# Queries and keys from batch 2 on: cast in DRAM and transposed by DMA instead of by TensorE, and a wider gap between output tiles of the second layer

## The chip, the cores and the metric

The kernel runs on one core of one Trainium2 chip. The metric is the device time of one execution in microseconds (us). A core has TensorE (PE in the profile, its weight loads PEld), VectorE (DVE), ScalarE (ACT), GpSimd (POOL) and SyncE (SP), which here only issues DMAs; each works through its own instructions in order and waits on semaphores for the others. A lower time is better.

## The reference

Attention with a bias by relative distance, then a two-layer network with a squared ReLU:

```python
B, H, S, D = 8, 8, 576, 64             # batches, heads, positions, head size
scores = q @ k.T / 8 + bias_table[bucket(|i - j|)]      # per batch and head
attn = exp(scores - max) / sum
x = (attn @ v), heads side by side      # 4608 tokens x 512
h = maximum(x @ w_in, 0)                # 512 -> 2048
out = (h * h) @ w_out                   # 2048 -> 512, float32
```

Inputs are float32; the kernel computes in fp16 with float32 sums.

## The kernel before

A batch is handled as four pairs of heads and two halves of 288 queries. `run(h)` issues one half: h = 0 to 15, batch h // 2, half ic = h % 2. For each pair it walks a list of slots. There are five score slots (four blocks of 128 keys and one of 64: TensorE writes the transposed scores `st` to PSUM, ScalarE takes the exponential to `et` or `em`, VectorE multiplies a band near the diagonal by the bias table), two slots for the product with v (`pv`) of the pair before, and, in the second half of a batch, one slot "t" that prepares the same pair of the next batch. After each slot `feed` issues pieces of the two network layers, by due times in steps, 28 steps to a half: `ffn1` (line 354, tiles `hps`, ReLU `rt` by ScalarE, square into `g_sb` by VectorE) and `ffn2` (line 376). An output tile of `ffn2` is 16 matmuls into the one PSUM tile `yps`, issued two at a time in eight pieces; VectorE then scales it to `y` (line 382), which frees `yps` for the next tile, and SP stores it. The due times of the eight pieces leave `F2_GAP` steps between the last piece of one tile and the first of the next (`layer2`).

Everything of one engine is issued in the order of this program, so a late operand stops all that stands behind it on that engine.

How q and k come in: SP loads both as float32 with heads side by side (`load_qk`, line 112: ten DMAs a batch with 256-byte rows). GpSimd casts them to fp16 tiles `qh` and `kh` (`cast_qk`, line 162; 32 casts a batch), one half ahead of their use. In slot "t", `transposes(p)` has TensorE transpose five blocks of q and five of k into one of the two PSUM slots that the scores also use (line 235), and VectorE copies the result out in four pieces (lines 238 to 241): q to `qt`, and k to `kz`, where the two heads of a pair lie in different partitions with zeros beside them, so that one 128-row matmul gives one head's scores. v is loaded by SP and cast by GpSimd piece by piece (`cast_v`, line 169); the casts of w_out for the second layer (line 196) stand in h = 2. The memory pools: `qt` five slots, `kz` five tiles, score PSUM two slots, `yps` one.

Of the kernel before, what the change touches and what calls it, by code (L numbers as in the profile page):

```python
# [13 lines left out]
FP16 = mybir.dt.float16  # L14
# [6 lines left out]
B, H, S, D = 8, 8, 576, 64  # L21
# [6 lines left out]

STEP, AFTER1, AFTER2 = 28, 9, 3

F2_GAP = 2.0
F2_PACE = STEP * 16 / 288
F2_START = 5 * STEP + AFTER1 + AFTER2 - 48 * F2_PACE
TILES = [(0, 1), (2, 3), (4, 5), (6, 7, 8)]
# [15 lines left out]
def kernel(  # L50
# [10 lines left out]
    nc = tc.nc  # L61
    assert (_bucket(np.arange(128, S)) == NBK - 1).all()

    def io(ins):
        tc.keep_in_program_order(ins)
        return ins
# [5 lines left out]
    eye = np.eye(128, dtype=np.float16)  # L72
    id_d = nc.inline_tensor(np.concatenate([eye, eye[::-1]], axis=1), name="c_id")
    tdram = nc.dram_tensor("t_bias", (H, 512), FP16, kind="Internal")

    single = ctx.enter_context(tc.tile_pool(name="single", bufs=1))
    stg_pool = ctx.enter_context(tc.tile_pool(name="stg", bufs=1))
    ws_pool = ctx.enter_context(tc.tile_pool(name="ws", bufs=4))
    qt_pool = ctx.enter_context(tc.tile_pool(name="qt", bufs=5))
    et_pool = ctx.enter_context(tc.tile_pool(name="et", bufs=11))  # L80
    nr_pool = ctx.enter_context(tc.tile_pool(name="nr", bufs=2))
    em_pool = ctx.enter_context(tc.tile_pool(name="em", bufs=3))
    xt_pool = ctx.enter_context(tc.tile_pool(name="xt", bufs=2))
    rt_pool = ctx.enter_context(tc.tile_pool(name="rt", bufs=3))
# [22 lines left out]
    kzs = [single.tile([128, 2 * S], FP16, name=f"kz{i}") for i in range(5)]  # L107
# [3 lines left out]
    def sdma(eng, out_, in_):  # L111
        io(eng.dma_start(out=out_, in_=in_))  # L112


    stgs = {}

    def stage(b, names):
        stgs.setdefault(b, [None] * 3)
        for n in names:
            stgs[b]["qkv".index(n)] = stg_pool.tile([128, 5, 512], FP32, tag=n + "s", name=n + "s")  # L120

    def load_qk(b, h0, n, w, eng=nc.sync):
        t, src = stgs[b][w], (q, k)[w]
        for tt in range(4) if n > 2 else ():
            sdma(
                eng,
                t[:, tt, ds(64 * h0, 64 * n)].rearrange("p (h d) -> p h d", d=D),
                src[b, h0 : h0 + n, ts(tt, 128), :].transpose([1, 0, 2]),
            )
        for h in range(h0, h0 + n) if n <= 2 else ():  # L130
            sdma(eng, t[:, 0:4, ts(h, D)], src[b, h, 0:512, :].rearrange("(t p) d -> p t d", p=128))
        sdma(
            eng,
            t[0:64, 4, ds(64 * h0, 64 * n)].rearrange("p (h d) -> p h d", d=D),
            src[b, h0 : h0 + n, 512:576, :].transpose([1, 0, 2]),
        )

    def load_v(b):
        vs = stgs[b][2]
        for tt in range(4):  # L140
            sdma(
                nc.sync,
                vs[:, tt, :].rearrange("p (h d) -> p h d", h=8),
                v[b, :, ts(tt, 128), :].transpose([1, 0, 2]),
            )
        for e in range(2):
            sdma(
                nc.sync,
                vs[ds(64 * e, 64), 4, :].rearrange("p (h e d) -> p h e d", e=2, d=64)[
                    :, :, e, :  # L150
                ],
                v[b, e::2, 512:576, :].transpose([1, 0, 2]),
            )
# [36 lines left out]
    def load_w_out(u):  # L190
        ws[u] = ws_pool.tile([128, 2, 512], FP32, tag="ws", name="ws")
        sdma(nc.sync, ws[u], moe_w_out[ds(u * 256, 256), :].rearrange("(a p) c -> p a c", p=128))
# [22 lines left out]
    def table(hp):  # L215
        for e in range(2):
            tp = psF.tile([128, 512], FP32, tag=f"f{e + 1}", name="tbp")
            io(
                nc.tensor.matmul(
                    tp[:, 0:384], flip_sb, tr[hp // 2][:, 2 * (hp % 2) + e, :], start=True, stop=True  # L220
                )
            )
            io(nc.vector.tensor_copy(out=tb_sb[:, 2 * hp + e, :], in_=tp[:, 0:384]))
            io(nc.gpsimd.tensor_copy(out=tm_sb[ds(64 * e, 64), hp, :], in_=tb_sb[0:64, 2 * hp + e, 0:192]))


    qts, ets, bands = {}, {}, []

    def transposes(p):
        b, hp = divmod(p, 4)  # L230
        qh, kh = h16s
        tp = psS.tile([128, 2, 1024], FP16, tag="s", name="tp")
        for w, src in ((0, qh), (1, kh)):
            for t in range(5):
                io(nc.tensor.transpose(tp[:, w, ts(t, 128)], src[:, t, ts(hp, 128)], id_sb))  # L235
        qt = qt_pool.tile([128, S], FP16, tag="qt", name="qt")
        kz = kzs[p % 5]
        io(nc.vector.tensor_copy(out=kz[0:64, 0:S], in_=tp[0:64, 1, 0:S]))
        io(nc.vector.tensor_copy(out=qt, in_=tp[:, 0, 0:S]))
        io(nc.vector.tensor_copy(out=kz[64:128, S + 64 : 2 * S], in_=tp[64:128, 1, 0:512]))  # L240
        io(nc.vector.tensor_copy(out=kz[64:128, S : S + 64], in_=tp[64:128, 1, 512:S]))
        qts[p] = (qt, kz)
# [151 lines left out]
    def layer2():  # L394
        for h in range(2 * B):
            for _ in ffn2(h):
                nq[0] += 1
                m, n = divmod(nq[0], 8)
                yield F2_START + 8 * m * F2_PACE + n * (8 * F2_PACE - F2_GAP) / 7

# [6 lines left out]
    def feed(t):  # L407

        while streams:
# [11 lines left out]
            name=nc.get_next_instruction_name(),  # L421
# [12 lines left out]
    for h0 in (2, 4):  # L434
        for w in range(2):
            load_qk(0, h0, 2, w)
# [49 lines left out]
    def run(h):  # L486

        nonlocal pending
        b, ic = divmod(h, 2)
        slots = []  # L490
        for hp in range(4):
            p = 4 * b + hp
            slots.append(("unit", hp))
            slots += [("s", p, jt, ic) for jt in range(3)]
            nt = p + 1 if h == 0 and hp < 3 else p + 4 if ic == 1 and b + 1 < B else None
            if nt is not None and h > 0:
                slots.append(("t", nt))
            if h == 0 and hp == 1:
                slots.append(("table",))
            slots += [("pv",), ("pv",)]  # L500
            if nt is not None and h == 0:
                slots.append(("t", nt))
            slots += [("s", p, jt, ic) for jt in range(3, 5)]
            slots.append(("end", p, ic))
        n_real = sum(s_[0] not in ("end", "unit", "table") for s_ in slots)
        at = 0
        for s_ in slots:
            if s_[0] == "end":
                pending = pv(s_[1], s_[2])
                continue  # L510
            if s_[0] == "table":
                for i in range(4):
                    table(i)
                    for p, f in [x for x in bands if x[0] == i]:
                        f()
                bands.clear()
                continue
            if s_[0] == "unit":
                hp = s_[1]
                if b + 1 < B:  # L520
                    if ic == 0 and b > 0 or ic == 1 and b == 0:
                        for w in range(2):
                            for e in range(2):
                                cast_qk(b + 1, w, 2 * hp + e, 1, nc.gpsimd)
                if h in (0, 1):
                    cast_w_in(4 * h + hp)
                if b + 1 < B:
                    u = max(0, 4 * ic + hp - 1) if b else max(0, 5 * h + hp - 6) * 2
                    n = (4 * ic + hp) if b else max(0, 5 * h + hp - 5) * 2
                    q7 = 7 if b else 6  # L530
                    for t, e in V_PIECES[min(10, u * 10 // q7) : min(10, n * 10 // q7)]:
                        cast_v(b + 1, t, e)
                if h == 2:
                    cast_w_out(2 * hp)
                    cast_w_out(2 * hp + 1)
                if h == 0:
                    if hp < 2:
                        io(nc.vector.memset(kzs[3 + hp].bitcast(FP32), 0.0))
                continue
            if s_[0] == "s":  # L540
                scores(*s_[1:])
            elif s_[0] == "t":
                transposes(s_[1])
            elif pending is not None:
                next(pending, None)
            at += 1
            tick()
            feed(STEP * (h + at / n_real))

    for h in range(2 * B):  # L550
        b, ic = divmod(h, 2)
        if h == 1:
            for u in range(4):
                load_w_out(u)
        if ic == 1 and b + 2 < B:
            stage(b + 2, "qk")
            for w in range(2):
                load_qk(b + 2, 0, 8, w)
        if ic == 0 and 0 < b < B - 1:
            stage(b + 1, "v")  # L560
            load_v(b + 1)
        if h == 2:
            for u in range(4, 8):
                load_w_out(u)
        run(h)
    for _ in range(2):
        next(pending, None)
# [34 lines left out]
```

## Time and profile before

| | us |
|---|---|
| median of three runs | 508.09 (505.37 to 520.13) |
| the profiled execution | 505.52 |
| its span, first to last instruction | 503.7 |
| around the span | 1.8 |

The profile is of one execution. It gives each instruction's start and length on its engine, and infers from semaphores what ended each wait. "Idle before" a group is time in which its engine stood still just ahead of it. Matmuls are pipelined: the pace of a row of matmuls is seen from the start of one piece to the start of the next, and is shorter than the length shown.

### The profile page before, as it was taken

The page shows a single profiled execution, that of the slowest core. Times are in us where ns is not written, and L with a number is a line of the kernel's source. Part 1 is how long each engine was busy: PE and PEld are TensorE (multiplying, and loading weights), DVE is VectorE, ACT ScalarE, POOL GpSimd, SP SyncE. Part 2 cuts the span into 40 slices and gives each one's busy share as a digit, 9 for nine tenths or more (in the row PEclk, how much of TensorE's full clock was granted, in tenths as well). Part 3 has the DMA queues.
Part 4 walks back from the last instruction along what each step waited for, and adds up shares of the span by engine and source line. Part 5 has one row for each costly group of instructions (what it writes and reads, how often), then busy time and mean ns, then how long its engine had stood idle before and what let it go on. Part 6 is the DMA issues. An engine that isn't in the chain of part 4 may idle for free.

```text
span 503.7 us, 9141 instructions
## 1 busy us (share of the span) xinstructions
PE 447.2 (89%) x3145; PEld 296.4 (59%) x3145; DVE 317.3 (63%) x825; ACT 337.9 (67%) x774; POOL 134.4 (27%) x369
## 2 busy tenths in 40 slices
PE   2576888899999989999999989999999999997996
PEld 1244565576566755676666756666666666664552
DVE  4668979976656765576656765576657664454331
ACT  2357788677776677777776777677776777775330
POOL 4586829820601251020601251020600000000000
PEclk9999999999999999999999999999999999999899
DMA  8998999835019150905019150915000000000101
GB/s 168 226 253 242 266 199 235 146 81 101 20 43 196 37 108 7 208 31 109 22 36 195 38 101 22 199 33 115 22 25 19 30 17 20 31 34 1 40 32 75
DMA packets 123149, 47.61 MB, mean 95 GB/s; under 512 B 114040, under 2 KB 114240, under 8 KB 123104
## 3 DMA queue, kind: packets, MB, share of 16 engines
q1 hardware_dynamic: 121360, 45.86, 40.4%
q0 software_dynamic: 256, 0.79, 0.6%
q10 hardware_dynamic: 1488, 0.40, 0.4%
q8 instruction: 24, 0.39, 0.4%
q14 instruction: 21, 0.17, 0.1%
HBM read 37.59 MB, written 9.45 MB: 93 GB/s over the span
## 4 chain that ended last, share of the span: by engine, by line
PE 63%; ACT 10%; DVE 9%; SPq 6%; DMA 5%; issue 4%; POOL 1%; DVEq 0%; POOLq 0%; ACTq 0%
PE yps L376 21%; PE hps L354 19%; PE pv L310 12%; PE st L254 9%; SPq L112 6%; ACT et L263 4%; DMA vs<-in_v_dram 3%; DVE y L382 3%; ACT r L318 2%; PE tp L235 2%; DVE xt L327 2%; ACT rt L363 2%; DVE g_sb L364 2%; DMA ks<-in_k_dram 1%; DVE et L277 1%
## 5 line engine op out<-in xcount | busy, mean ns | idle before, releaser
L376 PE MATMUL yps<-w_out_sb,g_sb 128*128 128x512 f16 x576 | 168.1, 381 | 16.0 <-DVE y L382 16.0
L363 ACT ACTIVATE rt<-hps 128x288 f16<-128x288 f32 x256 | 104.5, 408 | 104.9 <-PE hps L354 102.6
L263 ACT ACTIVATE et<-st 128x576 f16<-128x576 f32 x256 | 162.7, 646 | 15.4 <-PE st L254 14.8
L354 PE MATMUL hps<-xt,w_in_sb 128*128 128x288 f16 x1024 | 168.8, 287 | 2.8 <-DVE xt L327 1.9
L277 DVE TENSOR_TENSOR et<-et,tb_sb 128x512 f16<-128x512 f16 (+3 forms) x224 | 94.9, 429 | 98.0 <-ACT et L263 96.1
L364 DVE TENSOR_TENSOR g_sb<-rt 128x288 f16<-128x288 f16 x256 | 95.3, 373 | 53.3 <-ACT rt L363 49.3
L354 PEld LDWEIGHTS <-w_in_sb 128*128 128x128 f16 x1024 | 100.3, 98 | 47.4 <-issue 3.5
L254 PE MATMUL st<-qt,kz 128*128 128x288 f16 x512 | 104.1, 289 | 13.0 <-ACT et L263 10.4
L254 PEld LDWEIGHTS <-kz 128*128 128x128 f16 x512 | 50.2, 98 | 60.6 <-issue 25.4
L310 PE MATMUL pv<-et,vz 128*128 128x288 f16 x512 | 84.5, 288 | 1.0 <-DVE xt L327 1.0
L376 PEld LDWEIGHTS <-g_sb 128*128 128x128 f16 x576 | 56.2, 98 | 38.8 <-issue 19.7
L310 PEld LDWEIGHTS <-vz 128*128 128x128 f16 x640 | 62.3, 98 | 26.4 <-DVE xt L327 1.5
L162 POOL CAST qh<-qs 128x256 f16<-128x256 f32 (+1 forms) x116 | 36.2, 347 | 95.5 <-DMA qs<-in_q_dram 54.4
L327 DVE TENSOR_TENSOR xt<-pv,r 64x288 f16<-64x288 f32 x128 | 58.1, 454 | 5.1 <-ACT r L321 1.9
L169 POOL CAST vz<-vs 128x256 f16<-128x256 f32 (+1 forms) x80 | 34.6, 460 | 93.1 <-PE pv L310 84.5
L162 POOL CAST kh<-ks 128x256 f16<-128x256 f32 (+1 forms) x116 | 35.5, 341 | 26.1 <-DMA ks<-in_k_dram 22.4
L310 PE MATMUL pv<-em,vz 128*128 128x288 f16 x128 | 36.9, 288 | 0.3 <-DVE em L277 0.3
L317 ACT ACTIVATE r<-pv 64x288 f32<-64x288 f32 x64 | 26.1, 408 | 13.3 <-PE pv L310 11.8
L382 DVE TENSOR_SCALAR y<-yps 128x512 f32<-128x512 f32 x36 | 24.9, 691 | 10.2 <-PE yps L376 9.2
L318 ACT ACTIVATE r<-pv 64x288 f32<-64x288 f32 x64 | 25.8, 402 | 6.3 <-PE pv L310 5.0
L321 ACT ACTIVATE r<-r 128x288 f32<-128x288 f32 x64 | 28.3, 443 | 2.0
L271 ACT ACTIVATE em<-st 128x288 f16<-128x288 f32 x64 | 26.4, 412 | 2.7 <-PE st L269 2.7
(41 smaller groups left out, 186.0 us busy)
## 6 DMA issues: line engine op xcount, KB each, us to landing
out_dram<-y SPq DMA_DIRECT2D x36, 256.0 KB, 2.1
vs<-in_v_dram SPq DMA_DIRECT2D x32, 256.0 KB, 4.9
qs<-in_q_dram SPq DMA_DIRECT2D x24, 256.0 KB, 4.6
ks<-in_k_dram SPq DMA_DIRECT2D x24, 256.0 KB, 5.4
g_sb<-in_moe_w_in_dram SPq DMA_DIRECT2D x8, 512.0 KB, 5.5
ws<-in_moe_w_out_dram SPq DMA_DIRECT2D x8, 512.0 KB, 5.0
qs<-in_q_dram SPq DMA_DIRECT2D x22, 128.0 KB, 4.5
ks<-in_k_dram SPq DMA_DIRECT2D x20, 128.0 KB, 3.2
```

Of the source, the lines that this page charges most:

```text
L162: io(eng.tensor_copy(out=dst, in_=src))
L254: nc.tensor.matmul(st[:, e, 0:IC], kz[:, ds(640 * e + jt * 128, 128)], qt[:, ds(c0, IC)], start=True, stop=True,)
L263: io(nc.scalar.activation(out=et, in_=st[:, :, 0:IC], func=EXPF, scale=SCALE))
L277: io(nc.vector.tensor_tensor(out=sl, in0=sl, in1=tab, op=MULT))
L310: nc.tensor.matmul(pvs[e][:, 0:IC], vz[:, jt, 2 * hp + e, :], rhs, start=(jt == 0), stop=(jt == 4))
L318: io(nc.scalar.activation(out=r[64:128, :], in_=pvs[1][0:64, 0:IC], func=LNF))
L327: nc.vector.tensor_tensor(out=xt[o : o + 64, hp, ds(ic * IC, IC)], in0=pvs[e][o : o + 64, 0:IC], in1=r[o : o + 64, :], op=MULT,)
L354: nc.tensor.matmul(hps[:, 0:IC], w_in_sb[:, kk, ts(nt, 128)], xt[:, kk, ds(h % 2 * IC, IC)], start=(kk == 0), stop=(kk == 3),)
L363: io(nc.scalar.activation(out=rt, in_=hps[:, 0:IC], func=RELUF))
L364: io(nc.vector.tensor_tensor(out=g_sb[:, nt, o : o + IC], in0=rt, in1=rt, op=MULT))
L376: nc.tensor.matmul(yps, g_sb[:, nt, ts(m, 128)], w_out_sb[:, nt, :], start=(nt == 0), stop=(nt == 15))
L382: io(nc.vector.tensor_scalar_mul(out=y, in0=yps, scalar1=OSC))
```

## The change

From batch 2 on q and k take another way (`DMA_FROM = 2`). `halve(b)` issues 16 DMAs from GpSimd, one per head and tensor, each of 576 rows of 64 float32 values, which go to new fp16 tensors in DRAM (`d16`) with the heads side by side. It is called for batch 2 at the start of h = 2 and for batch b + 2 at the start of the second half of batch b. `turn(p)` takes the place of `transposes(p)`: SP issues two transposing DMAs, of 576 rows by 128 columns, one to `qt` and one to a new tile `kt` (two slots). The three copies that spread `kt` into `kz` (VectorE, SBUF to SBUF) are put off to the start of the next pair's list. The float32 loads, GpSimd's casts, TensorE's transposes and VectorE's four copies out of PSUM go for batches 2 to 7, 24 pairs in all. Slot "t" no longer counts as a slot for `feed` there. `F2_GAP` goes from 2 to 4 steps, with the tile's eight pieces set closer.

```diff
-F2_GAP = 2.0
+F2_GAP = 4.0
+
+DMA_FROM = 2
...
+    def halve(b):
+
+        for dst, src in zip(d16, (q, k)):
+            for h in range(H):
+                sdma(nc.gpsimd, dst.ap()[b, :, ts(h, D)], src[b, h])
+
+    def turn(p):
+
+        b, hp = divmod(p, 4)
+        qt = qt_pool.tile([128, S], FP16, tag="qt", name="qt")
+        kz = kzs[p % 5]
+        kt = kt_pool.tile([128, S], FP16, tag="kt", name="kt")
+        for out_, src in ((qt, d16[0]), (kt, d16[1])):
+            io(nc.sync.dma_start_transpose(out=out_, in_=src.ap()[b, :, ts(hp, 128)]))
+
+        def spread():
+            io(nc.vector.tensor_copy(out=kz[0:64, 0:S], in_=kt[0:64, :]))
+            io(nc.vector.tensor_copy(out=kz[64:128, S + 64 : 2 * S], in_=kt[64:128, 0:512]))
+            io(nc.vector.tensor_copy(out=kz[64:128, S : S + 64], in_=kt[64:128, 512:S]))
+
+        spreads.append(spread)
+        qts[p] = (qt, kz)
...
-        n_real = sum(s_[0] not in ("end", "unit", "table") for s_ in slots)
+        n_real = sum(s_[0] not in ("end", "unit", "table") and not (s_[0] == "t" and s_[1] >= 4 * DMA_FROM) for s_ in slots)
...
                 hp = s_[1]
-                if b + 1 < B:
+                while spreads:
+                    spreads.pop(0)()
+                if b + 1 < DMA_FROM:
...
             elif s_[0] == "t":
-                transposes(s_[1])
+                if s_[1] < 4 * DMA_FROM:
+                    transposes(s_[1])
+                else:
+                    turn(s_[1])
+                    continue
...
         if ic == 1 and b + 2 < B:
-            stage(b + 2, "qk")
-            for w in range(2):
-                load_qk(b + 2, 0, 8, w)
+            if b + 2 < DMA_FROM:
+                stage(b + 2, "qk")
+                for w in range(2):
+                    load_qk(b + 2, 0, 8, w)
+            elif b > 0:
+                halve(b + 2)
...
             for u in range(4, 8):
                 load_w_out(u)
+            halve(2)
```

On TensorE, between the end of the fourth output tile and the start of the fifth, before. `yps` is the output tile, `st` a score block, `hps` a piece of the first layer; weight loads alternate with the matmuls.

```order
L376 MATMUL yps<-w_out_sb,g_sb 128x512
L254 LDWEIGHTS kz_107
L254 MATMUL st<-qt,kz_107 128x288
...
L354 LDWEIGHTS w_in_sb
L354 MATMUL hps<-xt,w_in_sb 128x288
...
L254 LDWEIGHTS kz_107
L254 MATMUL st<-qt,kz_107 128x288
...
L376 MATMUL yps<-w_out_sb,g_sb 128x512
```

There are eight matmuls in that gap: two of `st`, four of `hps`, two of `st`. The same place of the changed kernel:

```order
L403 MATMUL yps<-w_out_sb,g_sb 128x512
L281 LDWEIGHTS kz_114
L281 MATMUL st<-qt,kz_114 128x288
...
L381 LDWEIGHTS w_in_sb
L381 MATMUL hps<-xt,w_in_sb 128x288
...
L296 MATMUL st<-qt,kz_114 128x288
L281 LDWEIGHTS kz_110
L281 MATMUL st<-qt,kz_110 128x288
...
L403 MATMUL yps<-w_out_sb,g_sb 128x512
```

Here fifteen matmuls stand in the gap: seven of `st` and eight of `hps`. Over the 29 gaps up to the last half the work between tiles was six to fourteen matmuls of 288 columns, some with ten transposes of 128 columns among them, and is now 15 to 26 matmuls of 288.

On GpSimd, at the start of h = 2, before: the last casts of v for batch 1 (`vz_113`), then q and k of batch 2, then the first casts of w_out.

```order
L169 CAST vz_113<-vs 64x4x64 x2
L162 CAST qh<-qs 128x4x64
L162 CAST qh<-qs 64x64
...
L162 CAST kh<-ks 128x4x64
L162 CAST kh<-ks 64x64
L196 CAST w_out_sb<-ws 128x512 x4
```

In the changed kernel, at the same place:

```order
L196 CAST vz_116<-vs 64x4x64 x2
L116 DMA q<-in_q_dram 576x64 x8
L116 DMA k<-in_k_dram 576x64 x8
L223 CAST w_out_sb<-ws 128x512 x4
L196 CAST vz_115<-vs 128x4x64
L223 CAST w_out_sb<-ws 128x512 x4
```

All 16 DMAs of batch 2 stand ahead of the first cast of w_out, and in h = 3, 5, 7, 9 and 11 another 16 stand ahead of the last six casts of v of the next batch.

On SP, where the transposes of batch 3 begin, the changed kernel has, in place of ten loads of q and k in one go:

```order
L116 DMA vs<-in_v_dram 64x4x64 x2
L116 DMA out_dram<-y 128x512 x2
L155 DMA_TRANSPOSE qt<-q 128x576
L155 DMA_TRANSPOSE kt<-k 128x576
L116 DMA out_dram<-y 128x512
L155 DMA_TRANSPOSE qt<-q 128x576
L155 DMA_TRANSPOSE kt<-k 128x576
```

The transposing DMAs stand between the stores of `y`, two for each pair, 48 in all.

## Rows read from the trace of the kernel before

**Rows 1.** The page, part 1: busy us (share of the span) xinstructions of each engine.

```profile
PE 447.2 (89%) x3145; PEld 296.4 (59%) x3145; DVE 317.3 (63%) x825; ACT 337.9 (67%) x774; POOL 134.4 (27%) x369
```

**Rows 2.** Busy by stretch, halves h = 4 to 14: length, engines, clock, DMA share, GB/s.

```profile
235.50:263.60 28.10, 26.02 (x176) 17.18 (x176) 17.23 (x45) 20.81 (x49) 8.57 (x26) 1.00 0.05 20
263.60:292.30 28.70, 27.89 (x218) 19.50 (x217) 20.06 (x58) 20.77 (x49) 5.09 (x16) 1.00 0.59 131
...
sum 312.40, PE 295.49 PEld 200.21 DVE 196.97 ACT 228.29 POOL 62.71; mean PE 26.86 PEld 18.20 DVE 17.91 ACT 20.75 POOL 5.70
```

**Rows 3.** The page, part 5: groups; count, busy us, mean ns, idle before and releaser.

```profile
L376 PE MATMUL yps<-w_out_sb,g_sb 128*128 128x512 f16 x576 | 168.1, 381 | 16.0 <-DVE y L382 16.0
L363 ACT ACTIVATE rt<-hps 128x288 f16<-128x288 f32 x256 | 104.5, 408 | 104.9 <-PE hps L354 102.6
L263 ACT ACTIVATE et<-st 128x576 f16<-128x576 f32 x256 | 162.7, 646 | 15.4 <-PE st L254 14.8
```

**Rows 4.** Line 382 (y): who waited for it, us in total, times.

```profile
  PE yps L376: 16.0, 19
```

**Rows 5.** Timeline, 94 to 97 us: start us, us, engine, line, operation, tiles, count.

```profile
94.44 0.44 PE L235 MATMUL tp<-ids_sb,qh 128*128 128x128 f16 x5
94.48 1.55 DVE L364 TENSOR_TENSOR g_sb<-rt 128x288 f16<-128x288 f16 x2
...
94.72 0.44 PE L235 MATMUL tp<-ids_sb,kh 128*128 128x128 f16 x5
...
94.99 0.65 PE L310 MATMUL pv<-et,vz 128*128 128x288 f16 x4
...
95.61 0.65 PE L354 MATMUL hps<-xt,w_in_sb 128*128 128x288 f16 x4
...
96.10 0.59 PE L376 MATMUL yps<-w_out_sb,g_sb 128*128 128x512 f16 x2
...
96.53 0.65 PE L310 MATMUL pv<-et,vz 128*128 128x288 f16 x4
```

**Rows 6.** Timeline, 237 to 239 us, in h = 8: the wait between two output tiles.

```profile
237.69 0.30 DVE L364 TENSOR_TENSOR g_sb<-rt 128x288 f16<-128x288 f16 x1
...
238.02 0.69 DVE L382 TENSOR_SCALAR y<-yps 128x512 f32<-128x512 f32 x1
...
238.76 0.59 PE L376 MATMUL yps<-w_out_sb,g_sb 128*128 128x512 f16 x2 [0.88 <-DVE y L382]
```

**Rows 7.** Groups by form: VectorE's copies out of PSUM after the transposes.

```profile
L238 DVE COPY kz<-tp 64x576 f16<-64x576 f16 x32 | 14.3, 448 | 7.9 <-PE tp L235 7.3
...
L239 DVE COPY qt<-tp 128x576 f16<-128x576 f16 x32 | 14.1, 440 | 0.0
...
L240 DVE COPY kz<-tp 64x512 f16<-64x512 f16 x32 | 13.7, 427 | 0.4
...
L241 DVE COPY kz<-tp 64x64 f16<-64x64 f16 x32 | 6.0, 187 | 0.0
```

**Rows 8.** DMA issues: KB each, median us from issue to landing.

```profile
out_dram<-y SPq DMA_DIRECT2D x36, 256.0 KB, 2.1
...
ks<-in_k_dram SPq DMA_DIRECT2D x24, 256.0 KB, 5.4
...
tr<-t_bias POOLq DMA_DIRECT2D x2, 384.0 KB, 6.6
```

**Rows 9.** Groups on GpSimd: its DMA instructions.

```profile
L112 POOL DMA_DIRECT2D tr<-t_bias x2 | 1.7, 856 | 2.3 <-DMA t_bias<-tv_sb 2.3
L112 POOL DMA_DIRECT2D t_bias<-tv_sb x1 | 0.7, 699 | 3.9 <-DVE tv_sb L204 3.9
```

**Rows 10.** Timeline, h = 2: GpSimd's casts.

```profile
62.78 1.93 POOL L169 CAST vz<-vs 128x256 f16<-128x256 f32 x4
...
76.68 2.28 POOL L196 CAST w_out_sb<-ws 128x512 f16<-128x512 f32 x4
```

**Rows 11.** Timeline, h = 2: TensorE's first matmuls of the second layer.

```profile
85.20 0.59 PE L376 MATMUL yps<-w_out_sb,g_sb 128*128 128x512 f16 x2
```

More of the change, by code (lines that the diff above doesn't have):

```diff
@@ L74 @@
     tdram = nc.dram_tensor("t_bias", (H, 512), FP16, kind="Internal")
+    d16 = [nc.dram_tensor(f"{n}16", (B, S, H * D), FP16, kind="Internal") for n in "qk"]
     single = ctx.enter_context(tc.tile_pool(name="single", bufs=1))
@@ L81 @@
     nr_pool = ctx.enter_context(tc.tile_pool(name="nr", bufs=2))
+    kt_pool = ctx.enter_context(tc.tile_pool(name="kt", bufs=2))
     em_pool = ctx.enter_context(tc.tile_pool(name="em", bufs=3))
@@ L112, in sdma @@
         io(eng.dma_start(out=out_, in_=in_))
-    stgs = {}
+    stgs, qts, spreads = {}, {}, []
     def stage(b, names):
@@ L224, in table @@
             io(nc.gpsimd.tensor_copy(out=tm_sb[ds(64 * e, 64), hp, :], in_=tb_sb[0:64, 2 * hp + e, 0:192]))
-    qts, ets, bands = {}, {}, []
+    ets, bands = {}, []
     def transposes(p):
```

## The prediction

> **What bounds the kernel now.** I read the page first, then the busy time by half of a batch, then the groups with long waits, then the timeline around two of them. TensorE is busy for 89% of the span, ScalarE for 67%, VectorE for 63% and GpSimd for 27% [rows 1]. In the halves h = 4 to 14 the eleven stretches add up to 312.4 us, so a half takes 28.4 us, in which TensorE is busy 26.9, ScalarE 20.8 and VectorE 17.9 on average; the DMA share is 0.59 at most in the two stretches shown [rows 2]. TensorE leads, but it is not full. At its own pace four matmuls of 288 columns take 0.49 us and two of 512 columns 0.43 us, start to start [rows 5]. A half has 36 score, 40 pv and 64 first-layer matmuls at 0.12 us and 36 of the second layer at 0.215 us: 16.8 + 7.7 = 24.5 us. A second half adds four sets of transposes at 0.55 us (94.44 to 94.99) [rows 5], so 26.7 us.
>
> The reader should see something odd in [rows 2]: the half with transposes (263.60 to 292.30) takes 28.7 us and the half without them (235.50 to 263.60) 28.1 us. The transposes cost 2.2 us of TensorE and yet the half is only 0.6 us longer. The reason is the other large wait. TensorE waits 16.0 us in 19 waits for `y`, which must be read out before the one `yps` tile is used again [rows 3, 4]. In h = 8 the last matmuls of a tile are followed by 0.96 us of other work (eight matmuls) and then 0.88 us of nothing [rows 6]. First halves have three such waits, in second halves the transposes and the four more slots partly fill the gap. So the two parts of the change have to be costed together: taking out the transposes alone would bring the waits for `y` to the second halves too.
>
> **The change part by part.** The sum is made against the profiled execution, 505.5 us, which is 0.5% under the median of 508.1.
>
> *TensorE's transposes.* 24 sets go, at 0.55 us: -13.2 us [rows 5]. They are on the path, since TensorE issues in order.
>
> *The gap.* In h = 8 the gap needed 0.96 + 0.88 = 1.84 us of work to hide `y` (0.69 us of VectorE, and the way to and from it) [rows 6]. By the order of the changed kernel, the 29 gaps up to the last half hold 15 to 26 matmuls of 0.12 us, 1.8 to 3.1 us, against 0.8 to 1.7 us before. So even the shortest just cover it. I leave 2 of the 16.0 us [rows 4], for times when VectorE comes to `y` late: -14 us. What is late next is ScalarE: in a gap of seven `st` matmuls (three full blocks and a small one) and eight `hps` it has 3 x 0.65 us plus three smaller ones of about 0.41 us [rows 3], 3.2 us of work against TensorE's 1.8 us. Two PSUM slots for scores and one for `hps` let TensorE run ahead by about as much; the bounds are 0 and, with 29 gaps at 0.5 us, 15 us. I take 0.1 us for each, +3 us.
>
> *VectorE.* A set loses four copies of 448, 440, 427 and 187 ns, 1.5 us [rows 7], and gets three from SBUF. These are at most 448 + 427 + 187 = 1.06 us and at least 3 x 0.19. VectorE gains 10 to 22 us in all, beside TensorE: 0. But the spread stands in VectorE's order, and if its `kt` has not landed everything behind it waits, the bands that `pv` needs and the squares. From SP's dispatch to the spread there are the two pv and two score slots, some 4 us at 28.4 us for 28 slots, and up to 3 us more, as SP may run ahead once the `qt` slot is free.
>
> *The transposing DMAs.* No such DMA is in the trace. Nearest are a contiguous store of 256 KB, landed in 2.1 us, and a load of 256-byte rows, 5.4 us with several in flight [rows 8]; each new one moves 147 KB. I take 3 us, nearer to the lone store, since they stand two at a time in a queue that is no longer filled by ten loads at once. Then 0.5 us of waiting in some of the 24 spreads, +1 us. At 5.4 us it matters whether they overlap (first rival).
>
> *The casting DMAs.* 96 on GpSimd. Two of its DMAs with 512 pieces (128 x 4) took 856 ns each, and one with 8 pieces 699 ns [rows 9], so 576 pieces should take 0.7 to 0.9 us; I take 0.86 us, 14 us a batch. At h = 2 GpSimd is through with v at 64.7 us, so w_out's casts start at 78.5 us, against 76.7 before [rows 10], with no casts of q and k between them. The first matmul that reads w_out starts at 85.2 us [rows 11]. Hidden: 0, and it would cost 1 us for each us by which 64.7 + 16d passes 85, that is, for d above 1.3 us. In later batches 16d and six casts of v (2.8 us, at 1.93 us for four [rows 10]) have a half and about 8 us more before `pv` needs the last piece: d up to 2.1 us costs nothing.
>
> A page of the Trainium skill, "SBUF — State Buffer", section "Who interferes with whom", says that a VectorE copy in a two-port mode and a GpSimd instruction shut each other out for a whole instruction, descriptor writing included. The trace shows such a meeting only for casts: two squares took 1.55 us beside casts of v, at 94.48, and one took 0.30 us in h = 8 [rows 5, 6]. By that rule up to half of the 72 spread copies would wait some 0.4 us for a casting DMA, 14 us of VectorE over six halves, most of it in its idle 10 us a half, and the sum would be some 2 us higher; the sum here leaves it out.
>
> *Sum.* 505.5 - 13.2 - 14 + 3 + 1 = 482 us. A second way: a half needs 24.5 us, keeps about 1.1 us of the waits that are not for `y` (28.1 - 24.5 - 3 x 0.85) and 0.6 us at its 2.25 gaps, 26.2 us. Twelve halves from 28.4 to 26.2 are 26 us, and h = 3 loses four sets and a wait or two, 3 us: 476 us. I take 480 us.
>
> **The rivals.**
> *The transposing DMAs do not keep pace (slower).* If they go through one at a time with L us each, the eight of a second half need 8L, against 26.2 us. Above L = 3.3 us VectorE stops at the spread and with it the program; six halves are longer by 8L - 26.2. At 3.9 us that is 30 us, which eats the whole gain, 510 us; at the 5.4 us of a load [rows 8], 17 us in each half, 582 us. For it: nothing in the trace shows that two overlap. Against it: plain loads do overlap, ten in a queue, and there are 4 to 7 us of slack for each pair. The Trainium skill, "VectorE: DVE Perf Modes", section "The three transpose paths", gives 1309 ns for a 128 x 128 transpose by DMA and 390 ns by TensorE; 4.5 such blocks in a row would be an estimate of 5.9 us, and 606 us. TensorE's pace here is 0.055 us a block [rows 5], far better than that page's figure, and no run here shows the other.
>
> *ScalarE takes over the gap.* The wait for `y` comes back as waits for exponentials, at the 15 us bound, and the transposes give only the 0.6 us by which halves with them are longer, plus the part of 16 us that stays released: 505.5 - 3.6 - 7 = 495 us. For it: ScalarE is at 20.8 of 28.4 us [rows 2] and would be at 80% in 26. Against it: its 20.8 us still fit with 5 us to spare.
>
> *GpSimd is late.* At d = 2 us the first reader of w_out is 11.5 us late, 492 us; at 3 us v is late by 17 us in five halves as well, near 590 us. The row at 856 ns [rows 9] speaks against it, but it is of pieces three times as long, to SBUF and with no cast.
>
> **How the numbers follow.** The forecast, 474 to 490 us around 480, has a chance of 0.66. ScalarE taking over has 0.12, half of it above 498. GpSimd late has 0.07: 0.03 faster, 0.02 within, 0.02 slower. The slow transposing DMAs have 0.15: 0.02 within and 0.13 slower. A measurement of this kernel tells about 2% from no change: 498 to 518 us around the median. Faster 0.66 + 0.06 + 0.03 = 0.75, same 0.06 + 0.02 + 0.02 = 0.10, slower 0.15. The range goes from 468 us (both ways too cautious) to 505 us; what is left out is the slow DMAs above and a few hundredths below.
>
> **What would show it.** Right: no `tp` matmuls after h = 1; TensorE's idle time before `yps` under 4 us in total; halves of 26 to 26.5 us, first and second alike; VectorE's wait before the first copy of a spread under 1 us each; the casting DMAs under 1 us each on GpSimd. Wrong: a large wait of VectorE for `kt`, which would be the first rival; TensorE waiting for ScalarE before `st` by 10 us more than now, the second; w_out's casts after 87 us, the third. Halves of unlike length, with the second ones long, would say that the DMA path and not TensorE sets the time.

## The result and the profile after

The changed kernel takes 483.9 us in the median of four runs (481.8 to 485.6), beside 512.7 us for the kernel before on the same chip (505.4 to 520.1 in four runs). Two of those four (517.4 and 520.1) fell in a slower state of the chip, and the ratio, here and below, is of fast runs alone: 0.955, with a 95% interval from 0.947 to 0.963, faster by 4.5%. The forecast was 480 us. The profiled execution took 483.91 us, its span is 482.0 us.

The busy times come first, from the page: the engines, then the granted clock of TensorE in 40 slices.

```profile
PE 430.4 (89%) x2905; PEld 283.8 (59%) x2905; DVE 282.9 (59%) x801; ACT 340.1 (71%) x774; POOL 136.5 (28%) x273
...
PEclk9779899999999999999999999999999999998899
```

TensorE has 240 instructions fewer than in [rows 1], the ten transposes of 24 pairs, and is busy for 16.8 us less; its share is 89% as before, now of a shorter span. Next come the halves h = 4 to 7 and the sum over h = 4 to 14, with the columns of [rows 2].

```profile
121.20:148.00 26.80, 25.39 (x175) 16.97 (x175) 16.75 (x48) 20.83 (x49) 13.69 (x26) 1.00 1.03 120
148.00:173.90 25.90, 25.52 (x176) 17.17 (x176) 15.31 (x51) 21.03 (x49) 0.00 (x0) 1.00 0.34 65
173.90:201.10 27.20, 25.82 (x179) 17.39 (x179) 16.73 (x47) 20.97 (x49) 14.28 (x26) 1.00 0.98 108
201.10:227.10 26.00, 25.64 (x177) 17.18 (x176) 15.52 (x51) 20.92 (x49) 0.00 (x0) 1.00 0.28 67
...
sum 291.80, PE 281.58 PEld 188.99 DVE 175.66 ACT 230.45 POOL 60.30; mean PE 25.60 PEld 17.18 DVE 15.97 ACT 20.95 POOL 5.48
```

The eleven halves went from 312.4 us [rows 2] to 291.8: 20.6 of the 21.7 us by which the span is shorter. The four lengths repeat to the end. Second halves, which held the transposes, are now the shorter ones, 26 us against 27. The start up to h = 4 (121.2 us, 121.8 before) and the tail after h = 14 (482.0 - 413.0 = 69.0 us, 69.5 before) gained almost nothing; what hides the start's gain is told further below. Where the time went shows in the groups, from the list of lines (busy, mean ns, idle before and its releasers).

```profile
L381 PE MATMUL hps<-xt,w_in_sb 128*128 128x288 f16 x1024 | 168.6, 288 | 5.4 <-ACT rt L390 3.4 <-DVE xt L354 1.9
L403 PE MATMUL yps<-w_out_sb,g_sb 128*128 128x512 f16 x576 | 166.6, 380 | 0.6 <-DVE y L409 0.6
...
L281 PE MATMUL st<-qt,kz 128*128 128x288 f16 x512 | 105.2, 288 | 17.6 <-ACT et L290 15.3 <-DVE qt L266 0.9 <-DVE kz L268 0.2
...
L158 DVE COPY kz<-kt 64x576 f16<-64x576 f16 x24 | 7.1, 297 | 6.4 <-DMA kt<-k 6.4
L159 DVE COPY kz<-kt 64x512 f16<-64x512 f16 x24 | 7.0, 291 | 0.3
L160 DVE COPY kz<-kt 64x64 f16<-64x64 f16 x24 | 4.2, 175 | 0.0
```

The 16.0 us before `yps` in [rows 3] are 0.6 us now. The waits for ScalarE are 15.3 us before `st` and 3.4 before `hps`; in the kernel before they are 10.4 and 0.8:

```profile
L354 PE MATMUL hps<-xt,w_in_sb 128*128 128x288 f16 x1024 | 168.8, 287 | 2.8 <-DVE xt L327 1.9 <-ACT rt L363 0.8
...
L254 PE MATMUL st<-qt,kz 128*128 128x288 f16 x512 | 104.1, 289 | 13.0 <-ACT et L263 10.4 <-DVE qt L239 0.9 <-DVE kz L241 0.4
```

The gap that [rows 6] show, now in h = 8, from the timeline:

```profile
228.90 0.69 DVE L409 TENSOR_SCALAR y<-yps 128x512 f32<-128x512 f32 x1
...
229.04 0.41 PE L281 MATMUL st<-qt,kz 128*128 128x288 f16 x2
...
229.64 0.59 PE L403 MATMUL yps<-w_out_sb,g_sb 128*128 128x512 f16 x2 [0.19 <-DVE y L409]
```

VectorE's 0.69 us are the same, but TensorE has score and first-layer matmuls up to 229.45, and what is left of 0.88 us is 0.19 us, one of three such waits. The new DMAs, in the list of issues (KB each where it is given, median us to landing) and in GpSimd's groups:

```profile
q<-in_q_dram POOLq DMA_DIRECT2D x48, 72.0 KB, 3.4
k<-in_k_dram POOLq DMA_DIRECT2D x48, 72.0 KB, 3.5
...
qt<-q SPq DMA_TRANSPOSE x24, 2.8
kt<-k SPq DMA_TRANSPOSE x24, 2.8
```

```profile
L116 POOL DMA_DIRECT2D k<-in_k_dram x48 | 30.3, 660 | 2.7 <-DMA q<-in_q_dram 2.6
L116 POOL DMA_DIRECT2D q<-in_q_dram x48 | 30.2, 644 | 0.0
```

A casting DMA holds GpSimd for 0.65 us, and the casts of w_out start at 76.43 us, where they started at 76.68 before [rows 10].

### The profile page after: what moved, and what is told of

Its sections match the earlier page's. It is cut to its first block, busy times and chain, and to the rows that moved or that the text cites. A ratio compares the mean times of both kernels' runs of the same rounds, so it can differ in the third digit from the quotient of the medians.

```text
span 482.0 us, 8553 instructions
## 1 busy us (share of the span) xinstructions
PE 430.4 (89%) x2905; PEld 283.8 (59%) x2905; DVE 282.9 (59%) x801; ACT 340.1 (71%) x774; POOL 136.5 (28%) x273
## 4 chain that ended last, share of the span: by engine, by line
PE 74%; ACT 8%; SPq 7%; DMA 4%; issue 3%; DVE 3%; POOL 1%; DVEq 0%; POOLq 0%
PE yps L403 25%; PE hps L381 24%; PE pv L337 13%; PE st L281 11%; SPq L116 7%; ACT et L290 3%; ACT rt L390 3%; DMA vs<-in_v_dram 2%; ACT r L345 2%; ACT r L344 2%; PE st L296 1%; DVE xt L354 1%; DVE y L409 1%; DMA ks<-in_k_dram 1%; DMA qs<-in_q_dram 1%
## 5 line engine op out<-in xcount | busy, mean ns | idle before, releaser
L304 DVE TENSOR_TENSOR et<-et,tb_sb 128x512 f16<-128x512 f16 (+3 forms) x224 | 89.0, 401 | 99.3 <-ACT et L290 97.9
L281 PE MATMUL st<-qt,kz 128*128 128x288 f16 x512 | 105.2, 288 | 17.6 <-ACT et L290 15.3
L391 DVE TENSOR_TENSOR g_sb<-rt 128x288 f16<-128x288 f16 x256 | 86.0, 336 | 57.1 <-ACT rt L390 53.7
L196 POOL CAST vz<-vs 128x256 f16<-128x256 f32 (+1 forms) x80 | 33.2, 444 | 191.6 <-DMA vs<-in_v_dram 77.5
L337 PE MATMUL pv<-et,vz 128*128 128x288 f16 x512 | 85.6, 291 | 1.0 <-DVE xt L354 1.0
L337 PEld LDWEIGHTS <-vz 128*128 128x128 f16 x640 | 63.4, 99 | 27.2 <-DVE xt L354 1.4
L344 ACT ACTIVATE r<-pv 64x288 f32<-64x288 f32 x64 | 26.1, 408 | 12.4 <-PE pv L337 10.9
L409 DVE TENSOR_SCALAR y<-yps 128x512 f32<-128x512 f32 x36 | 24.9, 691 | 11.1 <-PE yps L403 10.2
L116 POOL DMA_DIRECT2D k<-in_k_dram x48 | 30.3, 660 | 2.7 <-DMA q<-in_q_dram 2.6
L116 POOL DMA_DIRECT2D q<-in_q_dram x48 | 30.2, 644 | 0.0
## 6 DMA issues: line engine op xcount, KB each, us to landing
qs<-in_q_dram SPq DMA_DIRECT2D x16, 128.0 KB, 3.3
ks<-in_k_dram SPq DMA_DIRECT2D x14, 128.0 KB, 3.3
```

The costliest lines, as they stand in the source:

```text
L281: nc.tensor.matmul(st[:, e, 0:IC], kz[:, ds(640 * e + jt * 128, 128)], qt[:, ds(c0, IC)], start=True, stop=True,)
L304: io(nc.vector.tensor_tensor(out=sl, in0=sl, in1=tab, op=MULT))
L337: nc.tensor.matmul(pvs[e][:, 0:IC], vz[:, jt, 2 * hp + e, :], rhs, start=(jt == 0), stop=(jt == 4))
L344: io(nc.scalar.activation(out=r[0:64, :], in_=pvs[0][64:128, 0:IC], func=LNF))
L391: io(nc.vector.tensor_tensor(out=g_sb[:, nt, o : o + IC], in0=rt, in1=rt, op=MULT))
```

## The experiments

Two theories stood after the result. The theory of the prediction: TensorE sets the time, transposes and gap pay jointly, and the new way for q and k lies beside other work. Against it: the parts pay each for itself, or the new way costs something that is hidden in the halves of unlike length.

**The gap alone.** The kernel before, with one constant changed:

```diff
-F2_GAP = 2.0
+F2_GAP = 4.0
```

> The kernel before with F2_GAP at 4 alone. Joint theory (the wait for y and the transposes fill the same holes of TensorE): the 16.0 us of waits for y fall to 2, and 2 to 3 us come back as waits for ScalarE, so 492 to 495 us against 505.5, ratio 0.975 to 0.98; TensorE's transposes stay at 13.2 us. Rival (the gain comes from the transposes, the gap matters little): 501 us or more, ratio above 0.99.

Measured: 499.5 us, ratio 0.981 (0.974 to 0.988): in time between the two forecasts, by the ratio at the edge of the first. Two halves and the sum over h = 4 to 14:

```profile
126.50:153.30 26.80, 25.40 (x174) 16.97 (x174) 17.15 (x44) 20.83 (x49) 8.64 (x26) 1.00 0.34 75
153.30:181.40 28.10, 27.99 (x217) 19.48 (x217) 19.27 (x58) 20.82 (x49) 4.90 (x16) 1.00 0.60 122
...
sum 302.20, PE 293.33 PEld 200.25 DVE 195.95 ACT 229.07 POOL 61.99; mean PE 26.67 PEld 18.20 DVE 17.81 ACT 20.82 POOL 5.64
```

The gap gives 312.4 - 302.2 = 10.2 us. First halves are already those of the changed kernel, 26.8 us. Second halves are 28.1 us and full: TensorE is busy for 27.99 of them.

**The new way for q and k alone.** The changed kernel with the old gap:

```diff
-F2_GAP = 4.0
+F2_GAP = 2.0
```

> The changed kernel with F2_GAP back at 2. Joint theory: TensorE has 13.2 us less to do, but each second half then waits for y like a first half, the waits for y grow from 16 to about 28 us, and the time is 499 to 504 us, ratio 0.985 to 0.995. Rival (the two parts add up: the transposes are worth their 13.2 us by themselves): 491 to 493 us, ratio 0.97 to 0.975.

Measured: 493.7 us, ratio 0.972 (0.968 to 0.976). Two halves and the sum, then the wait for `y` in the list of waits (us in total, times, longest):

```profile
121.70:150.50 28.80, 26.00 (x176) 17.17 (x176) 16.85 (x47) 20.76 (x49) 14.16 (x26) 1.00 0.86 91
150.50:177.20 26.70, 25.78 (x178) 17.22 (x177) 15.61 (x51) 20.82 (x49) 0.00 (x0) 1.00 0.36 72
...
sum 303.30, PE 284.36 PEld 188.87 DVE 176.77 ACT 228.43 POOL 61.15; mean PE 25.85 PEld 17.17 DVE 16.07 ACT 20.77 POOL 5.56
```

```profile
PE yps L403 <- DVE y L409: 16.8, 15, 1.6
```

In the eleven halves it gives 312.4 - 303.3 = 9.1 us, and 10.2 + 9.1 = 19.3 against 20.6 for both; for the whole kernel it is 1.9% and 2.8% against 4.5%. The gains add up, and the joint theory falls. Without the transposes the waits for `y` did not move to the second halves. In h = 4 they are 2.7 us and in h = 6 2.0, in h = 5 0.8 and in h = 7 none; in the kernel before, h = 5 has 0.5 us and h = 7 none as well. By the order of this kernel's instructions, at 0.12 us a matmul, the gap of 2 steps holds 0.8 to 1.3 us of work in first halves, but 1.3 to 1.7 in second ones. Where ten transposes stood in a gap of the kernel before, five `pv` products stand here, since slot "t" no longer counts for `feed`.

**No new way at all, and no old one.** The casting DMAs, transposing DMAs and spreads are left out; batches 2 to 7 use the q and k tiles of batch 1, so that part of the computation is not done.

```diff
-                    turn(s_[1])
+                    qts[s_[1]] = qts[s_[1] - 4]
...
-            elif b > 0:
-                halve(b + 2)
...
-            halve(2)
```

> The changed kernel without any bringing in of q and k from batch 2 on: no casting DMAs, no transposing DMAs, no spreading copies; the batches reuse batch 1's q and k, so scores of later batches are computed from the wrong operands at the same size. If the new way is hidden beside TensorE, 481 to 484 us, the changed kernel's time less 0 to 3 us. If waiting for it (6.4 us of VectorE for kt) or its place on GpSimd and VectorE is paid for: 478 us or less.

Measured: 483.8 us, ratio 0.952 (0.948 to 0.956). Two halves and the sum:

```profile
121.30:148.10 26.80, 25.38 (x175) 16.96 (x175) 16.18 (x45) 20.83 (x49) 4.10 (x10) 1.00 0.32 74
148.10:174.00 25.90, 25.53 (x176) 17.18 (x176) 13.81 (x42) 21.02 (x49) 0.00 (x0) 1.00 0.15 40
...
sum 291.80, PE 281.57 PEld 188.97 DVE 163.17 ACT 230.42 POOL 19.77; mean PE 25.60 PEld 17.18 DVE 14.83 ACT 20.95 POOL 1.80
```

To a tenth of a microsecond these are the halves of the changed kernel, although VectorE is busy for 12.5 us less and GpSimd for 40.5 us less. So from h = 4 on the whole way by DMA is hidden, and the halves of 26 and 27 us are unlike for another reason.

**How much of it could be hidden.** Three runs load the new way. In the first each transposing DMA goes twice, once to a spare tile; in the second each casting DMA goes twice; in the third the spread stands right behind its DMA instead of at the next pair.

```diff
-            io(nc.sync.dma_start_transpose(out=out_, in_=src.ap()[b, :, ts(hp, 128)]))
+            spare = kt_pool.tile([128, S], FP16, tag="sp", name="spare")
+            for o_ in (spare, out_):
+                io(nc.sync.dma_start_transpose(out=o_, in_=src.ap()[b, :, ts(hp, 128)]))
```

> The changed kernel with every transposing DMA issued twice, first into a spare tile that nobody reads. In the changed kernel one takes SP 1.17 us and lands 2.8 us after issue; VectorE waits 6.4 us in all for kt. If such DMAs overlap and have slack, the last of four lands about 3 x 1.17 + 2.8 = 6.3 us after the first is issued, VectorE's wait for kt grows to 20 to 50 us and the time to 484 to 488 us. If they go through one at a time (4 x 2.8 = 11 us a pair, 45 us in a second half of 26): 570 us or more.

Measured: 488.6 us, ratio 0.962 (0.953 to 0.972), just above the first forecast. From the list of waits and that of the issues:

```profile
DVE kz L160 <- DMA kt<-k: 49.6, 20, 5.4
```

```profile
qt<-q SPq DMA_TRANSPOSE x24, 3.2
```

Of h = 4 to 14, the second halves, with eight further transposes each, are longer by 0 to 1.2 us. VectorE's wait for `kt` grew from 6.4 us to 49.6 in 20 spreads, and little of it reached TensorE. The four DMAs of a pair still landed after 2.8 to 3.2 us in the median, so more than one is under way at a time.

```diff
                 sdma(nc.gpsimd, dst.ap()[b, :, ts(h, D)], src[b, h])
+                sdma(nc.gpsimd, d16x.ap()[b, :, ts(h, D)], src[b, h])
```

> The changed kernel with every casting DMA issued twice, the second into a DRAM tensor that nobody reads: 32 instead of 16 on GpSimd for each batch, at 0.65 us each. If GpSimd's place is hidden in the later halves and only h = 2 feels it, the casts of w_out start some 12 us later than at 76.4 us, near the first use at 89, and the time is 484 to 490 us with the halves h = 4 to 14 unchanged at 26.5 us. If GpSimd's DMAs hold up VectorE (the shared port) or v: halves longer by 1 us or more, 495 us or more.

Measured: 487.8 us, ratio 0.958 (0.953 to 0.963). The halves h = 4 and 5:

```profile
123.70:152.80 29.10, 25.49 (x174) 16.96 (x174) 18.77 (x56) 21.00 (x49) 21.12 (x38) 1.00 1.53 145
152.80:178.70 25.90, 25.55 (x176) 17.18 (x176) 16.10 (x50) 21.03 (x49) 3.82 (x9) 1.00 0.75 87
```

From h = 5 on they stay at 25.9 to 27.2 us. h = 2, 3 and 4 are longer, by 1.2, 2.5 and 2.3 us: there the doubled DMAs of two batches and the casts of w_out follow each other on GpSimd. The casts of w_out start at 86.6 us, 10.2 later, and TensorE waits for them by 1.2 us in all; the rest of the lengthening was not followed to its cause.

```diff
                     turn(s_[1])
+                    spreads.pop(0)()
```

> The changed kernel with the three spreading copies put right behind their two DMAs in the program, without the slots between. If the slack of 4 to 7 us is what hides the DMAs, VectorE now waits 2 to 4 us for each of the 24 kt (50 to 90 us in all), the second halves grow by 2 to 8 us each and the time is 495 to 530 us. If SP runs far enough ahead or VectorE's idle time takes it: 484 to 488 us.

Measured: 507.9 us, ratio 1.001 (0.995 to 1.007): no faster than before. Two rows of the list of waits, and TensorE in two stretches of h = 11:

```profile
DVE kz L158 <- DMA kt<-k: 52.4, 12, 6.1
...
PE hps L381 <- DVE xt L354: 11.9, 4, 4.1
```

```profile
326.50:333.90 7.40, 4.41 (x30) 2.75 (x29) 1.45 (x7) 4.19 (x10) 0.00 (x0) 1.00 0.79 117
333.90:340.70 6.80, 5.83 (x22) 3.23 (x22) 3.36 (x13) 1.88 (x4) 0.00 (x0) 0.50 0.00 1
```

VectorE waits for `kt` about as long as in the kernel with doubled transposes (52.4 us beside 49.6), but now right in front of `xt` and the bands, which TensorE soon needs: it waits for `xt` by up to 4.1 us at a time. And the stall costs twice: after a stretch in which TensorE was busy for 4.41 of 7.40 us, its clock was granted at half, the lower level of 1.2 GHz, for the next 6.8 us. One line of order, four slots of slack for each pair, is worth as much as the whole change.

**Other gaps.** The changed kernel with 3 and with 6 steps:

```diff
-F2_GAP = 4.0
+F2_GAP = 3.0
```

> The changed kernel with F2_GAP at 3. By the order there are 1.1 to 2.4 us of work between two tiles against 1.8 to 3.1 us at a gap of 4 and 0.8 to 1.7 us at 2. The waits for y come to 3 to 6 us (16.8 at 2, 0.6 at 4), the waits of scores for ScalarE lie between 9.3 and 15.3: 484 to 488 us, no better than 4. If ScalarE is already the larger cost at 4, less than 482 us.

> The changed kernel with F2_GAP at 6. If the wait for y is used up at 4 (0.6 us left) and ScalarE is what a longer gap meets, waits of scores and of the first layer for ScalarE grow by 3 to 8 us: 486 to 492 us. If the gap were still what limits: 481 us or less.

Measured: 487.3 us with 3 steps (ratio 0.958, 0.952 to 0.965) and 492.4 us with 6 (0.968, 0.961 to 0.975). With 3 the waits for `y` are back at 8.3 us, and those for ScalarE before `st` are 12.6:

```profile
PE st L281 <- ACT et L290: 12.6, 24, 1.1
...
PE yps L403 <- DVE y L409: 8.3, 12, 1.1
```

With 6 the first are gone and the second are the most of any, 22.0 us, as its groups say:

```profile
L403 PE MATMUL yps<-w_out_sb,g_sb 128*128 128x512 f16 x576 | 164.0, 381 | 0.0
L281 PE MATMUL st<-qt,kz 128*128 128x288 f16 x512 | 105.6, 289 | 23.8 <-ACT et L290 22.0 <-DVE qt L266 0.9 <-DVE kz L268 0.4
```

Each step of gap trades VectorE's waits against ScalarE's. Beside the ratio of 0.955 with 4 steps these are 0.3 and 1.3 points higher, within or near the width of the intervals, so the times alone do not rank 3 and 4. The halves tell it more sharply: 27.0 us on average with 3, 27.1 with 6 and 26.5 with 4.

**Batch 1 the new way too.** `DMA_FROM` goes to 1, and `halve(1)` replaces the first loads of q and k for batch 1.

```diff
-DMA_FROM = 2
+DMA_FROM = 1
...
-    stage(1, "qk")
+    halve(1)
...
-        for w in range(2):
-            load_qk(1, h0, 4, w)
```

> Batch 1's queries and keys go the new way too (the casting DMAs right at the start in place of two float loads and their TensorE transposes). Theory (the halves from h = 4 on have nothing left that the new way pays for, only the start has): halves from h = 4 on as in the changed kernel, 25.9 to 27.2 us by turns; the stretch up to h = 4 shorter by what batch 1's transposes took, 0 to 4 us; 479 to 485 us in all. Rival (the first transposing DMAs stand behind the other loads of the start, so VectorE waits for them in h = 0 or 1): the stretch up to h = 4 longer by over 2 us, 486 us or more.

Measured: 490.7 us, ratio 0.967 (0.957 to 0.976). The rival's number held, but not by its wait. The halves are 25.9 to 27.2 us again, and h = 4 starts at 128.0 instead of 121.2. From the list of waits in h = 1 (39.2 to 77.4 us), and GpSimd's timeline:

```profile
PE hps L381 <- POOL w_in_sb L213: 8.6, 1, 8.6
```

```profile
40.24 0.63 POOL L116 DMA_DIRECT2D k<-in_k_dram  x1 [3.30 <-DMA q<-in_q_dram]
...
52.12 2.28 POOL L213 CAST w_in_sb<-g_sb 128x512 f16<-128x512 f32 x4
```

The casting DMAs stand ahead of the casts of the first layer's weights on GpSimd, which stops between two of them for an earlier one to land. In h = 1, which takes 38.2 us where it took 32.0, the granted clock is 0.78 on average, beside 0.95 in the changed kernel; how much of the loss is the clock's was not separated. This is the third rival's mechanism, GpSimd late, in another place.

**Every fourth ReLU by VectorE.** To see whether the remaining 15.3 + 3.4 us are ScalarE's fullness:

```diff
-            io(nc.scalar.activation(out=rt, in_=hps[:, 0:IC], func=RELUF))
+            if nt % 4 == 3 and not alone:
+                io(nc.vector.tensor_scalar_max(out=rt, in0=hps[:, 0:IC], scalar1=0.0))
+            else:
+                io(nc.scalar.activation(out=rt, in_=hps[:, 0:IC], func=RELUF))
```

> Every fourth ReLU of layer 1 goes to VectorE. Theory (after the change TensorE's remaining waits in the halves, st for et and hps for rt, 23 us in all, are ScalarE's fullness): ScalarE falls from about 340 to some 315 us, those two waits fall together by a third or more, 474 to 482 us. Rival (those waits are the order's, a single exponential or ReLU late, and VectorE is as late as ScalarE at the moved pieces, behind its reductions for the bands): hps then waits for VectorE, halves 26.5 us or longer, 484 to 495 us.

Measured: 555.7 us, ratio 1.096 (1.084 to 1.108), far above both forecasts. From its groups, its list of waits, and the timelines of VectorE and TensorE in h = 4:

```profile
L281 PE MATMUL st<-qt,kz 128*128 128x288 f16 x512 | 107.7, 294 | 17.2 <-ACT et L290 15.2 <-DVE qt L266 0.9 <-DVE kz L268 0.2
...
L391 DVE TENSOR_SCALAR rt<-hps 128x288 f16<-128x288 f32 x58 | 26.5, 457 | 1.6
```

```profile
PE hps L381 <- DVE rt L391: 62.2, 51, 4.3
```

```profile
137.43 0.46 DVE L304 TENSOR_TENSOR et<-et,tb_sb 128x576 f16<-128x576 f16 x1 [1.56 <-ACT et L290]
...
140.95 0.45 DVE L391 TENSOR_SCALAR rt<-hps 128x288 f16<-128x288 f32 x1
...
141.45 0.40 PE L381 MATMUL hps<-xt,w_in_sb 128*128 128x288 f16 x1 [2.81 <-DVE rt L391]
```

58 pieces at 457 ns, on an engine that is busy for 55% of the span, made the kernel 72 us longer than the changed one. VectorE is not idle in such a wait. It had stood still for 1.56 us for an exponential, and then works without a break through ten pieces (multiplications, `xt`, a square, `y`, a spread) before it comes to the ReLU; up to 4.3 us pass before the one `hps` tile is free. TensorE's clock fell as well, to 0.96 on average over h = 4 to 14, where it is 1.00 in the changed kernel. ScalarE has 13 us less to do in a span that is 77 us longer, and TensorE's wait for `et` is 15.2 us as before. So this wait looks like one of the order, several exponentials asked for in a row with two slots, and not of ScalarE's fullness. That is not shown: a run with the same span and a faster ScalarE was not made.

## Why the prediction held, point by point

*Transposes.* 13.2 us were costed for 24 sets. Between the gap alone and the changed kernel lies only the way of q and k: 302.2 - 291.8 = 10.4 us for the 20 sets of h = 4 to 14, 0.52 us each where [rows 5] gave 0.55, and h = 3 is 26.1 us against 28.1. In total 12.4 us. As the new way is hidden, this is the price of the old one. Right.

*The gap.* Costed at -14 us, and +3 for ScalarE, so -11; measured -10.2 in eleven halves and -1.9 in h = 3 (28.1 us against 30.0), so -12.1. The net is right, its terms less so. Of the waits for `y` 0.6 us stayed where 2 were left. In the changed kernel ScalarE took back 4.9 us before `st` and 2.6 before `hps`, 7.5 us against 3, so that term was sized too small by 4.5 us. In the eleven halves of the gap alone, 13.6 us of waits for `y` went and 6.0 of waits for ScalarE came, which would be 7.6 us of the 10.2; TensorE was also busy for 2.2 us less (295.5 and 293.3), which no term held and whose cause is open. So it is partly luck that the net came out. ScalarE's 7.5 us are within the bounds of 0 and 15 us, and the rival on ScalarE, all 15 us, did not come.

*That both parts have to be costed together.* This step failed. The equal halves in [rows 2] were read as one mechanism, the transposes filling the gap, without which the waits for `y` would come to the second halves. They were two numbers that happen to be near each other: 2.2 us of transposes in second halves, and the waits for `y` in first halves, where the gap held too little other work. With the transposes gone, `pv` products filled the gap of the second halves in their place. The sum was unharmed only because it added both terms in full.

*The transposing DMAs.* 3 us were taken, 2.8 were measured in the median, and they overlap. The stall at the spread is 6.4 us in 5 waits, where 0.5 us in some of the 24 were taken. The longest is 2.0 us, so "under 1 us each" was wrong, and all of it was covered, so the +1 was not needed. The first rival fell with the doubled transposes: one at a time, 16 of 2.8 us would be 45 us in a second half, and it took 25.9 to 27.1. The figure of the Trainium skill in "VectorE: DVE Perf Modes", "The three transpose paths", from which 5.9 us were estimated, does not fit: 4.5 blocks landed in 2.8 us. Nearer is "Advanced Engine Details and Errata", "X-Bar Transpose (TRN2)", by which a transposing DMA is as fast as a regular one: a store of 256 KB lands in 2.1 us here [rows 8], and q and k loads of 128 KB in 3.3 in the trace after.

*The casting DMAs.* 0.86 us were taken from pieces of [rows 9], 0.65 measured. Hidden, as said; w_out's casts came at 76.4 us where 78.5 was forecast.

*VectorE.* 0.76 us a spread, against 0.57 to 1.06. On its lock with GpSimd by the Trainium skill ("SBUF — State Buffer", "Who interferes with whom"), which the sum left out: the first copy took 292 to 303 ns in all 24 spreads, so none was held up. The casting DMAs run mostly in first halves and most spreads in second ones, and none of the 72 copies stands within 0.2 us of an instruction of GpSimd, so this is no test of the rule. In h = 6 the 16 squares averaged 362 ns beside casting DMAs, and 306 without them: 0.9 us in a half, in VectorE's idle time, and the half took 27.2 us both ways.

*Sum.* 482 us was the sum, 23.2 us below the profile before; the span fell by 21.7. By parts: the gap -12.1, the transposes -12.4, nothing for the stall at the spread, the start up to h = 3 +3.3 (95.1 us, 91.8 before), the tail -0.5. So gap and transposes gave a little more than the sum, and the start, which the sum held at nothing, took that back. The second way, 476, gave a half 26.2 us, it took 26.5, and over twelve halves that is 4 us. It had taken three waits of 0.85 us for `y` out of h = 8, where the list of waits has two:

```profile
PE yps L376 <- DVE y L382: 1.9, 2, 1.1
```

So the waits that are not for `y` were 28.1 - 24.5 - 1.9 = 1.7 us of a half and not 1.1. Halves of the same length were forecast, and first ones are 1 us longer. They hold what is left of TensorE's idle time (26.8 - 25.4 = 1.4 us, second halves 25.9 - 25.5 = 0.4): in h = 6 all of the 1.4 us that the list of waits names is `st` waiting for `et`. The forecast read long second halves as a sign of the DMA path; there was none.

*Where the rest is.* h = 3 gained 3.9 us, and the start up to h = 4 as a whole 0.6. In h = 0 and 1, whose work the change leaves as it was but for batch 2's loads, the profile after has two stretches at a low clock, the one before none:

```profile
18.00:29.00 11.00, 7.19 (x31) 3.63 (x30) 7.48 (x17) 2.22 (x6) 8.46 (x17) 0.54 0.94 228
...
49.00:53.00 4.00, 3.40 (x21) 2.26 (x18) 1.35 (x4) 0.32 (x1) 2.59 (x8) 0.57 1.10 254
```

The kernel with the gap alone shows that this need not be the change. Until the second layer begins, at 85.2 us in the kernel before [rows 11], its instructions are those of the kernel before, in the same order on every engine. The kernel before reached h = 2 at 66.8 us, the gap alone at 70.3 and the changed kernel at 70.8. The first two, from the start to there:

```profile
0.00:66.80 66.80, 41.23 (x275) 25.54 (x276) 47.66 (x105) 36.63 (x77) 43.55 (x101) 1.00 0.92 228
```

```profile
0.00:70.30 70.30, 42.25 (x276) 27.19 (x277) 46.61 (x106) 37.09 (x77) 43.06 (x102) 0.90 0.94 225
```

The same work took 3.5 us longer, at a granted clock of 0.90 on average. So executions of the same instructions differ there by about as much as the start lost, and the profile before was a quick one. How much of this is the clock is open: the kernel with a gap of 6, whose profile has no such stretch, reached h = 2 at 68.5 us.

## What to carry to other kernels

Two halves of equal length need not have one cause: put one part of a change back at a time, and see whether the gains add up before explaining them jointly. Work that goes to a DMA and an engine with time to spare cost nothing here, where its result is asked for late; the place of the wait in the consumer's order, not the duration of the transfer, decided here between 484 and 508 us. A busy share says little about where an engine can take work: VectorE at 59% had no place for a ReLU, GpSimd at 28% none for sixteen DMAs ahead of a cast that TensorE waited for. And before a part of the span is put down to a change, see by how much executions of the same instructions differ there.

## What the runs showed of the hardware that was not expected

- TensorE's clock fell to its lower level in mid-kernel in the third loading run, each time behind a stall for `kt` of 5.6 to 5.9 us: in three places from h = 3 to h = 13, the longest for 6.8 us. Between h = 4 and h = 14 no other profile shows that but the one with VectorE's ReLUs, where TensorE waited for those.
- Transposing DMAs of 576 x 128 land in 2.8 us in the median, in 3.2 at most when there are twice as many of them, and in 3.7 at most when there are twice as many casting DMAs.
- The same instructions, from the first to the start of h = 2, took 66.8 us in one execution and 70.3 in another, at a granted clock of 1.00 and 0.90 on average.
- DMAs of 576 rows of 64 values with a cast, from DRAM to DRAM, hold GpSimd for 0.65 us each and land 3.4 us after their issue, longer than the 2.1 us of a contiguous store, which the list of issues has at 256 KB against their 72.
